# One-core attention and state-space kernel: VectorE's list re-ordered at three places, the first weight copies divided differently, and two attention steps masked by a 0/1 product on GpSimd

## The chip, the core and the metric

The kernel runs on one core of a Trainium2 chip. The metric is the device time of one execution in microseconds (us). Before the change it is 133.39 us, the median of three runs (132.92 to 133.72).

## The reference

Two independent computations over 2048 tokens of width 448; their outputs stand side by side.

```python
# A: 16 heads of 28, each token looks at 8 keys: itself and 7 earlier ones, 2 apart
qkv = (x @ wqkv).reshape(B, S, 3, H, Dh)...
idx = pos[:, None] - (jnp.arange(8) * 2)[None, :]
logits = jnp.where(mask, einsum("bhsd,bhswd->bhsw", q, k[idx]) * scale, -1e9)
a = einsum("bhsw,bhswd->bhsd", softmax(logits), v[idx])... @ wo
# B: a diagonal complex recurrence over the tokens (state h of 448)
Lam_bar = jnp.exp(dt * Lam)
B_bar = ((Lam_bar - 1.0) / Lam)[:, None] * Bmat
h = Lam_bar * h + x[t] @ B_bar.T            # for t in range(2048)
y = 2.0 * real(h @ Cmat.T) + x * Dskip
return concatenate([a, y], -1)
```

## The kernel before

**Tiling.** Even and odd tokens are kept apart ("par" 0 and 1), so that a key distance of 2 is a distance of 1 in either half. Each half has 1024 tokens, in eight blocks b of 128. The attention of a block works on all keys of the same block as a dense 128x128 product per head and lets only a band of 8 through; queries at the start of a block, whose keys lie partly in the block before, are done by a ninth block of borders (b = 8). The recurrence runs over pairs of tokens in two halves hf of 512 pairs, on VectorE's scan instruction, in four groups k of state rows.

**The order.** Every instruction comes from a named step, and the string ORDER lists the steps; each engine executes its part in that order. A token such as `n4.V1` is step n4, on V (VectorE), with PSUM bank pair 1; A is ScalarE, P TensorE, G GpSimd, S the DMA queue of SyncE. The names that matter here:

- `xt0a`, `xt0b`, `xt1` to `xt3` transpose x on TensorE and `xe0a` and so on copy it to xA; `s1v`, `s2v` (lines 486 to 492) copy the v columns of the weights between the two partition halves, and the v steps (`v0e`, `v0o`; lines 351 to 366) multiply by them.
- `k..`, `q..`, `v..` are the projections, `ke`, `qe`, `ve` their copies out of PSUM.
- `s{b}{par}` makes the scores of a block: four mask matmuls (line 645) write a large negative number outside the band into PSUM, sixteen matmuls (line 649) add the products of keys and queries. `x{b}{par}` is the exponential on ScalarE into one of three buffers P (line 671), `a{b}{par}` the product with v (line 680), whose 29th column gives the sum of the weights. `n{b}` divides on VectorE (lines 691, 692), and a step `ot` transposes the result by DMA.
- `b{k}{hf}` makes the input of the recurrence on TensorE (line 727), `be` copies it, `ri` rotates it with two products (lines 742, 743) and two sums (744, 745), `sc` scans (line 755), `ro` rotates back into h (764 to 767). The lines for k = 3 are 747 to 750 and 771 to 774.
- `c1{m}`, `c2{m}` mix the output weights on VectorE (line 540) from products that `tc..` makes on GpSimd or ScalarE (line 534); `g0` to `g2` combine weights on TensorE (782, 784) and `ge0`, `ge1`, `gp2`, `ge2` (809, 819) take them out.
- `y{t}` makes the recurrence's output for 128 pairs of tokens: 7 matmuls with h for the even tokens (line 851), 4 with Gm (854), 7 with h for the odd ones. Ahead of it `xd{t}` (line 841) writes x times Dskip into its bank. `ye` copies the result, `yo` sends it. `w{t}`, `we`, `wo` do the same for the attention.

In front of `y0` and `y1` stand `n8`, `n4`, `n5` in VectorE's list, because their banks are those that a50, a80 and y use. `y5` is the first y that reads the last rotated group, `ro01`.

Of the kernel before, what the change touches and what calls it, by code (L numbers as in the profile page):

```python
# [37 lines left out]
s11.P tc23.G n0.V1 k5t.P0 x11.A k5f.P0 wtx2.S c24.V a10.P1 ri00.V tc21.G qt3.S ke5.A0 s20.P a11.P1 x20.A q7t.P0 xb1.S  # L38
q7f.P0 n1.V1 s21.P qe7.A0 c23.V k6f.P1 x21.A c21.V tc22.G k6t.P1 sc000.V a20.P0 qt4.S ke6.A1 s30.P sc001.V a21.P0
tc20.A kt6.S b20.P1 c22.V x30.A n2.V0 tc25.G kt4.S ro00.V kt5.S s31.P be20.A1 b11.P0 x31.A ot0.S c25.V ri20.V qt5.S  # L40
b31.P1 be11.A0 qt6.S c20.V sc200.V s40.P be31.A1 vg1.S b01.P0 tc12.A tc16.V qt7.S x40.A c16.V c12.V tc15.G ot1.S
sc201.V tc10.A s41.P be01.A0 c10.V a30.P1 a31.P1 c15.V tc14.A b21.P0 vg2.S n3.V1 x41.A tc11.G c14.V ot3.S kb.G c11.V
tc13.A s50.P ot2.S be21.A0 c13.V tc26.G a40.P1 ro20.V x50.A g1.P0 xol.G a41.P1 ge1.A0 s51.P ri11.V g0.P0 x51.A n4.V1
s80.P ge0.A0 c26.V ot4.S a50.P1 sc110.V x80.A a51.P1 wol.S g2.P0 n5.V1 gp2.A0 s60.P ge2.V0 x60.A a80.P1 ot5.S xd1.V0
n8.V1 y1.P0 sc111.V ot8.S xd0.V1 ro11.V s61.P y0.P1 x61.A ri21.V ye1.A0 yo1.S oc0.A a60.P0 sc210.V ye0.A1 yo0.S a61.P0
s70.P n6.V0 w3t.P1 x70.A w3f.P1 sc211.V ot6.S w0f.P0 we3.A1 wo3.S ro21.V w0t.P0 oc1.A s71.P we0.A0 wo0.S w4f.P1 x71.A
ri31.V w5f.P0 w5t.P0 w4t.P1 sc310.V w1t.P2 we4.A1 wo4.S w2t.P3 w1f.P2 we5.A0 wo5.S xd3.V1 w2f.P3 ro31.V we1.A2 wo1.S
a70.P0 we2.A3 wo2.S a71.P0 xd2.V2 y3.P1 n7.V0 xd5.V3 ot7.S ri01.V y2.P2 ye3.A1 yo3.S sc010.V oc2.A sc011.V w6f.P0
# [105 lines left out]
def kernel(  # L154
# [129 lines left out]

    def consts_border():

        k7 = lambda m: m[:, 0:105].rearrange("p (b i) -> p b i", i=15)
        q7 = lambda m: m[:, 0:56].rearrange("p (b j) -> p b j", j=8)
        G.memset(m0, 1.0)
        sel(k7(m1), k7(m0), [[1, 7], [0, 15]], ALU.is_equal, 0.0, 0, -1)  # L290
        sel(k7(m2), k7(m0), [[0, 7], [1, 15]], ALU.is_equal, 0.0, 7, -1)
        G.tensor_tensor(mskb[0:32, 0, 0:105], m1[:, 0:105], m2[:, 0:105], ALU.add)
# [40 lines left out]
    def evac(e, o, i):  # L333
        if e == "A":
            ACT.copy(o, i)  # L335
        elif e == "G":
            G.tensor_copy(o, i)
        else:
            V.tensor_copy(o, i)  # L339
    step = {}  # L340
# [143 lines left out]

    for n, cols in (("v", VC), ("k", KC), ("q", QC)):
        def f(e, u_, cols=cols):
            evac(e, Wt[0:64, 4:7, cols], Wt[64:128, 0:3, cols])
        step["s1" + n] = f

        def f(e, u_, cols=cols):  # L490
            evac(e, Wt[64:128, 3:7, cols], Wt[0:64, 0:4, cols])
        step["s2" + n] = f
    for b_, (n, i, lo, hi) in enumerate((("0a", 0, 0, 3), ("0b", 0, 3, 7), ("1", 1, 0, 7), ("2", 2, 0, 7), ("3", 3, 0, 7))):
        def xt(b_=b_, w=hi - lo):
            return held_by("x")[b_ % 3][:, 0, :].bitcast(BF16)[:, 0:128 * w].rearrange("p (k t) -> p k t", k=w)

        def f(e, u_, xt=xt, i=i, lo=lo, hi=hi):
            for k in range(lo, hi):
                PE.transpose(xt()[:, k - lo, :], xn[:, i, 128 * k:128 * k + 128], eye[:])
# [134 lines left out]
    for place, b in enumerate(SEQ):  # L634
        main_b = b < BORDERS
        ring = 2 * place - (BORDERS in SEQ[:place])
        for par in range(2 if main_b else 1):
            c0, n = (0, 128) if b == 0 else (8, 120)
            Pt_ = Pb[(ring + par) % len(Pb)]

            def f(e, u_, b=b, par=par, n=n, c0=c0):
                s4 = held_by("s")[0]
                tk = slice(128 * b, 128 * b + 128)
                for g in range(4):
                    PE.matmul(s4[:, g, 0:4 * n].rearrange("p (s q) -> p s q", s=4), msk[32 * g:32 * g + 32, 0, :],
                              msk[32 * g:32 * g + 32, 1:2, c0:c0 + n].to_broadcast((32, 4, n)), start=True, stop=False, skip_group_check=True)
# [73 lines left out]
    for hf in range(2):  # L720
        for k in range(4):
# [15 lines left out]
            def f(e, u_, k=k, hf=hf):  # L737
# [8 lines left out]
                else:  # L746
# [2 lines left out]
                    V.tensor_tensor(v[0:64, 0], ra[0:64, 0], ra[64:128, 1], ALU.add)  # L749
                    V.tensor_tensor(v[64:128, 0], ra[64:128, 0], ra[0:64, 1], ALU.subtract)  # L750
            step[f"ri{k}{hf}"] = f
            for i in range(len(ms)):
                def f(e, u_, k=k, hf=hf, i=i):
                    m = k + 4 * i
                    V.tensor_tensor_scan(rs[0][:, i], p["r2"][:, k:k + 1].to_broadcast((128, HALF)), rv[0][:, i],  # L755
                                         0.0 if hf == 0 else ini[:, m:m + 1], ALU.mult, ALU.add)
# [223 lines left out]
```

## Time and profile before

| what | value |
|---|---|
| median of three runs | 133.39 us |
| the profiled execution | 133.22 us |
| its span | 131.4 us |
| granted TensorE clock | 1.00 |
| busy: TensorE, VectorE, ScalarE, GpSimd | 124.2, 107.1, 86.7, 48.1 us |
| GpSimd busy after 77.3 us | none |

The span is the time between the first and the last instruction of the profile. In rows of the timeline the first number is the start, the second the time from the first start to the last end, then come engine, line, operation, output and inputs, shapes and a count; a bracket says how long the engine stood idle before and what ended it. PE is TensorE, PEld its weight loads, DVE VectorE, ACT ScalarE, POOL GpSimd.

### The profile page before, as it was taken

Reading aid. Unit: us, or ns where it says so; the run is one execution under the profiler, and the core shown is the slowest. Engines: PE = TensorE matmul, PEld = TensorE weight load, DVE = VectorE, ACT = ScalarE, POOL = GpSimd, SP = SyncE. Lnnn points to the kernel's source line nnn. Section 1 sums busy time; section 2 is a strip of 40 time slices with the busy share of each in tenths; the row PEclk is TensorE's granted clock in tenths of the full one; section 3 lists DMA queues with packets and bytes.
Section 4 is the critical chain, followed back from the end, with each engine's and each line's share of the span. In section 5 each row is a group of like instructions: output and inputs, shape, how many; then the busy total and the mean of one; then the engine's idle time right before and its main releaser. Section 6 shows DMA issues by size and latency. Waiting matters only on the chain.

```text
span 131.4 us, 3138 instructions
## 1 busy us (share of the span) xinstructions
PE 124.2 (94%) x1226; PEld 63.5 (48%) x1226; DVE 107.1 (81%) x225; ACT 86.7 (66%) x91; POOL 48.1 (37%) x75
## 2 busy tenths in 40 slices
PE   7999999999999999899999998799999999999970
PEld 2654443443444466454445556545644654445540
DVE  2467999999898999999998999999999999870000
ACT  3348878987999879968698967608697523222230
POOL 7998900799851906560077850000000000000000
PEclk9999999999999999999999999999999999999999
DMA  4999998899779995898879967990452652422222
GB/s 98 373 299 223 246 114 164 121 250 204 166 120 200 227 134 86 157 205 200 178 159 148 203 123 260 181 205 14 138 145 71 209 145 70 140 70 72 70 72 80
DMA packets 54594, 20.83 MB, mean 158 GB/s; under 512 B 46830, under 2 KB 54208, under 8 KB 54576
## 3 DMA queue, kind: packets, MB, share of 16 engines
q1 hardware_dynamic: 53424, 18.70, 68.1%
q0 software_dynamic: 656, 1.50, 4.1%
q10 hardware_dynamic: 496, 0.40, 0.9%
q8 instruction: 11, 0.18, 0.6%
q14 instruction: 7, 0.06, 0.2%
HBM read 5.30 MB, written 3.86 MB: 70 GB/s over the span
## 4 chain that ended last, share of the span: by engine, by line
PE 62%; DVE 23%; issue 5%; DMA 3%; POOL 2%; ACT 1%; SPq 0%; DVEq 0%
PE U L362 16%; PE U L851 11%; PE early L362 8%; PE U L727 6%; PE late L851 4%; PE U L854 3%; PE U L360 3%; DVE O L692 3%; DVE natW L540 3%; DMA Wt<-in_A_wqkv_dram 3%; DVE C L540 3%; DVE rs L755 2%; POOL wtmp L534 2%; PE late L362 2%; PE early L360 2%
## 5 line engine op out<-in xcount | busy, mean ns | idle before, releaser
L671 ACT ACTIVATE P<-s 128x1920 bf16<-128x1920 f32 (+1 forms) x16 | 28.6, 1785 | 5.7 <-PE s L649 5.6
L727 PE MATMUL U<-xB,WT 128*128 128x512 bf16 x98 | 22.3, 380 | 0.0
L362 PE MATMUL U<-Wt,xA 128*128 128x448 bf16 x90 | 19.9, 355 | 0.7 <-DVE O L692 0.4
L362 PEld LDWEIGHTS <-xA 128*128 128x128 bf16 x144 | 12.9, 98 | 14.9 <-issue 4.4
L335 ACT CAST ys<-U 128x896 bf16<-128x896 f32 (+1 forms) x11 | 9.5, 871 | 12.0 <-PE U L851 9.2
L534 POOL TENSOR_SCALAR wtmp<-CT,p_pah 128x448 f32<-128x448 bf16 x6 | 12.6, 2107 | 11.2 <-DVE natW L540 6.4
L851 PEld LDWEIGHTS <-h 128*128 128x128 bf16 x105 | 10.0, 98 | 9.2 <-DVE U L841 0.2
L727 PEld LDWEIGHTS <-WT 128*128 128x128 bf16 x98 | 9.2, 98 | 10.7 <-DMA xB<-in_B_x_dram 0.2
L362 PE MATMUL early<-Wt,xA 128*128 128x448 bf16 x54 | 11.8, 354 | 0.0
L335 ACT CAST u<-U 128x1024 bf16<-128x1024 f32 (+1 forms) x8 | 7.2, 905 | 4.6 <-PE U L727 4.5
L692 DVE TENSOR_TENSOR O<-U,rcs 128x896 bf16<-128x896 f32 (+1 forms) x9 | 9.8, 1091 | 0.3
L851 PE MATMUL U<-natW,h 128*128 128x448 bf16 x42 | 9.0, 353 | 0.1
L755 DVE TENSOR_TENSOR_SCAN rs<-p_r,rv 128x512 bf16<-128x512 f32 x7 | 9.0, 1304 | 0.0
L755 DVE TENSOR_TENSOR_SCAN rs<-p_r,ini,rv 128x512 bf16<-128x512 f32 x7 | 8.8, 1275 | 0.0
L680 PE MATMUL U<-Vt,P 128*128 128x29 bf16 x256 | 8.2, 176 | 0.6 <-DVE O L692 0.6
L680 PEld LDWEIGHTS <-P 128*128 128x128 bf16 x256 | 7.6, 96 | 2.0 <-issue 0.7
L335 ACT CAST ys<-late 128x896 bf16<-128x896 f32 (+2 forms) x6 | 4.3, 718 | 6.1 <-PE late L851 5.6
L362 PE MATMUL U<-wo,OT 128*128 128x448 bf16 x36 | 7.6, 353 | 0.0
L851 PE MATMUL U<-C,h 128*128 128x448 bf16 x35 | 7.4, 353 | 0.0
L534 POOL TENSOR_SCALAR wtmp<-CT,p_pag 128x448 f32<-128x448 bf16 x2 | 4.2, 2081 | 8.4 <-DVE C L540 8.4
L339 DVE COPY Wt<-Wt 64x1344 bf16<-64x1344 bf16 (+1 forms) x5 | 3.7, 736 | 4.1 <-DMA Wt<-in_A_wqkv_dram 4.1
L335 ACT CAST Nx<-U 128x896 bf16<-128x896 f32 x7 | 6.4, 908 | 1.0 <-PE U L360 1.0
(198 smaller groups left out, 233.9 us busy)
## 6 DMA issues: line engine op xcount, KB each, us to landing
out_dram<-ys SPq DMA_DIRECT2D x12, 224.0 KB, 2.5
tmpB<-in_A_x_dram SPq DMA_DIRECT2D x4, 224.0 KB, 3.6
xo<-in_B_x_dram POOLq DMA_DIRECT2D x1, 896.0 KB, 6.7
out_dram<-ys SPq DMA_DIRECT2D x7, 112.0 KB, 1.8
Wt<-in_A_wqkv_dram SPq DMA_DIRECT2D x1, 672.0 KB, 6.0
wo<-in_A_wo_dram SPq DMA_DIRECT2D x2, 336.0 KB, 4.4
natW<-in_B_B_re_dram SPq DMA_DIRECT2D x1, 336.0 KB, 6.0
natW<-in_B_B_im_dram SPq DMA_DIRECT2D x1, 336.0 KB, 7.3
```

What stands on the lines that cost most here:

```text
L335: ACT.copy(o, i)
L360: PE.matmul(ps(u_)[j], x()[r, 3, c], w()[r, 3], start=first, stop=not first, skip_group_check=True)
L362: PE.matmul(ps(u_)[j], x()[:, 4 * j + k, c], w()[:, 4 * j + k], start=(k == 0 and first), stop=(k == 2 and not first), skip_group_check=True)
L534: (G if e == "G" else V).tensor_scalar(view(held_t[name][:]), src(), scale(), None, ALU.mult)
L540: V.scalar_tensor_tensor(view(dst()), src(), scale(), view(t[:]), ALU.mult, ALU.add)
L671: ACT.activation(pv[:, :, :, c0:128], s4[:, :, 0:4 * n].rearrange("p g (s q) -> p g s q", s=4), ACTF.Exp, scale=SCALE)
L680: PE.matmul(U[u_][:, q, 29 * hd:29 * hd + 29], P[:, hd // 4, hd % 4, :], Vt[:, b, q, hd, :], start=(hd == 0), stop=(hd == H - 1), skip_gro ...
L692: V.tensor_tensor(O[0:n, :].rearrange("p (t h d) -> p t h d", t=2, h=H), av[0:n, :, :, 0:DH], rc.unsqueeze(3).to_broadcast((n, 2, H, DH)), ...
L727: PE.matmul(U[u_][:, j, :], WT[:, i, 128 * m:128 * m + 128], xB[:, i, HALF * hf:HALF * hf + HALF], start=(i == 0), stop=(i == 6))
L755: V.tensor_tensor_scan(rs[0][:, i], p["r2"][:, k:k + 1].to_broadcast((128, HALF)), rv[0][:, i], 0.0 if hf == 0 else ini[:, m:m + 1], ALU.m ...
L851: PE.matmul(ps[:, 0:D], hb[:, m, lo:lo + 128], C1()[:, m, :] if par else natW[:, m, 0:D], start=(m == 0 and par == 0), stop=(m == 6 and pa ...
L854: PE.matmul(ps[:, 0:D], xB[:, k, tk], Gm[:, k, :], start=False, stop=(k == 3), skip_group_check=True)
```

## The change

1. **Start.** `xe0a` moves from ScalarE to VectorE. `s1v` copies one of its three rows of 448 columns (64 partitions); the other two become a step `s0v` on ScalarE, behind `xe0b`.
2. **ri00 in two.** `rp00` is its two products, `rq00` its two sums, and `n1` stands between them.
3. **ri11 and sc110.** `ri11` moves behind `n4`; `sc110` moves behind `n5`, `ge2`, `xd1` and `n8`.
4. **Products.** `s60` and `s70` leave out their four mask matmuls, so their first product matmul starts the sum. New steps `m60` and `m70` on GpSimd multiply P in place, 16 x 120 columns, by a 0/1 tile `band`, repeated over the 16 heads. `x60` and `x70` come before them, `a60` and `a70` behind. `band` is made at the start of GpSimd's step `cob` by a memset and two selects of 128x128.

```diff
-spin spin spin spin spin spin sps sps sps xt0a.P xt0b.P xe0a.A co0.G s1v.V xe0b.A sps sps v0e.P0 nw.S s2v.V nt.G sps
+spin spin spin spin spin spin sps sps sps xt0a.P xt0b.P xe0a.V co0.G s1v.V xe0b.A s0v.A sps sps v0e.P0 nw.S s2v.V nt.G
...
+    band = t_([128, 128], BF16, "band")
+    STEPS = {tok.partition(".")[0] for tok in ORDER.split()}
...
+        G.memset(band[:], 1.0)
+        sel(band[:], band[:], [[1, 128]], ALU.is_ge, 0.0, 0, -1)
+        sel(band[:], band[:], [[-1, 128]], ALU.is_ge, 0.0, 7, 1)
...
-            evac(e, Wt[0:64, 4:7, cols], Wt[64:128, 0:3, cols])
+            hi = 5 if cols == VC else 7
+            evac(e, Wt[0:64, 4:hi, cols], Wt[64:128, 0:hi - 4, cols])
...
+    step["s0v"] = lambda e, u_: evac(e, Wt[0:64, 5:7, VC], Wt[64:128, 1:3, VC])
...
-                for g in range(4):
+                masked = f"m{b}{par}" not in STEPS
+                for g in range(4 if masked else 0):
                     PE.matmul(s4[:, g, 0:4 * n]..., msk[32 * g:32 * g + 32, 0, :], ...
...
-                                  Qt[...], start=False, stop=(s == 3), skip_group_check=True)
+                                  Qt[...], start=(s == 0 and not masked), stop=(s == 3), skip_group_check=True)
...
+            def f(e, u_, P=Pt_, c0=c0):
+                pv = P[:].rearrange("p s g q -> p (s g) q")[:, :, c0:128]
+                G.tensor_tensor(pv, pv, band[:, c0:128].unsqueeze(1).to_broadcast((128, H, 128 - c0)), ALU.mult)
+            step[f"m{b}{par}"] = f
...
+            for nm, part in (("rp", 0), ("rq", 1)):
+                def f(e, u_, k=k, part=part):
+                    if part == 0:
+                        for o, s in ((ra, tab[:, 0, k, :]), (rb, tab[:, 1, k, :])):
+                            V.tensor_tensor(o[:], u[:, k:k + 5:4, :], s.unsqueeze(1).to_broadcast((128, 2, HALF)), ALU.mult)
+                    else:
+                        V.tensor_tensor(rv[0][:, 0], ra[:, 0], rb[:, 1], ALU.add)
+                        V.tensor_tensor(rv[0][:, 1], ra[:, 1], rb[:, 0], ALU.subtract)
+                step[f"{nm}{k}{hf}"] = f
```

How this stands in the engines' lists, at three places. VectorE at the start, behind its memsets, before:

```order
L339 COPY Wt<-Wt 64x3x448
L339 COPY Wt<-Wt 64x4x448
L339 COPY xA<-x_145 128x7x128
L339 COPY xA<-x_144 128x7x128
L339 COPY Wt<-Wt 64x3x448
```

and after, where the helper's copies are line 345:

```order
L345 COPY xA<-x_144 128x3x128
L345 COPY Wt<-Wt 64x448
L345 COPY Wt<-Wt 64x4x448
L345 COPY xA<-x_146 128x7x128
L345 COPY xA<-x_145 128x7x128
```

A copy of x (xe0a) has come in ahead, and the first weight copy (s1v) has a third of its columns.

VectorE around `n5` and `n8` before: c26 (natW), the scan sc110, n5 (rcs and the first O), ge2, xd1, n8 (a memset, rcs, the second O), the scan sc111, xd0.

```order
L540 SCALAR_TENSOR_TENSOR natW<-CT,p_sah,wtmp_125 128x448
L755 SCALAR_TENSOR_TENSOR rs_131<-p_r_321,ini,rv_130 128x512
L691 RECIPROCAL rcs<-U_94 128x32
L692 TENSOR_TENSOR O_1374<-U_94,rcs 128x896
L819 TENSOR_TENSOR Gm<-U_93,part 64x448
L841 TENSOR_TENSOR U_93<-xo 128x448
L688 MEMSET O_1435 32x448
L691 RECIPROCAL rcs<-U_94 56x32
L692 TENSOR_TENSOR O_1435<-U_94,rcs 56x896
L755 SCALAR_TENSOR_TENSOR rs_131<-p_r_321,ini,rv_130 128x512
L841 TENSOR_TENSOR U_94<-xo 128x448
```

The same place after (the scan is now line 778, the division 705 and 706, xd 864):

```order
L548 SCALAR_TENSOR_TENSOR natW<-CT,p_sah,wtmp_126 128x448
L705 RECIPROCAL rcs<-U_95 128x32
L706 TENSOR_TENSOR O_1378<-U_95,rcs 128x896
L842 TENSOR_TENSOR Gm<-U_94,part 64x448
L864 TENSOR_TENSOR U_94<-xo 128x448
L702 MEMSET O_1436 32x448
L705 RECIPROCAL rcs<-U_95 56x32
L706 TENSOR_TENSOR O_1436<-U_95,rcs 56x896
L778 SCALAR_TENSOR_TENSOR rs_132<-p_r_323,ini,rv_131 128x512
L864 TENSOR_TENSOR U_95<-xo 128x448
```

The scan sc110 has moved from ahead of n5 to behind n8. Ahead of these rows n4 and ri11 have changed places in the same way.

GpSimd's end of the list after: the copy of the border keys, the last product for c26, two loads of x and Dskip, and the two new products; before, the load of `flag` followed the two loads directly.

```order
L343 COPY Kb<-Kt 128x840
L542 TENSOR_SCALAR wtmp_126<-CT,p_pah 128x448
L931 DMA xo<-in_B_x_dram 128x8x448
L932 DMA xo<-in_B_Dskip_dram 128x448
L687 TENSOR_TENSOR P_84<-P_84,band 128x16x120
L687 TENSOR_TENSOR P_83<-P_83,band 128x16x120
L957 TENSOR_LOAD flag
```

Only these two instructions are new there; they wait for ScalarE's exponential, and a60 and a70 for them.

More of the change, by code (lines that the diff above doesn't have):

```diff
@@ L37 @@
 k2f.P1 qe4.A0 sc100.V s10.P qt2.S ke2.A1 b00.P0 sc101.V x10.A kt2.S ro10.V tc24.G kt7.S a00.P1 be00.A0 a01.P1 wtx6.S
[L38 to L41, printed above, removed]
+s11.P tc23.G n0.V1 k5t.P0 x11.A k5f.P0 wtx2.S c24.V a10.P1 rp00.V tc21.G qt3.S ke5.A0 s20.P a11.P1 x20.A q7t.P0 xb1.S
@@ L44 @@
[L44 to L48, printed above, removed]
@@ L49 @@
-ye2.A2 yo2.S ro01.V w6t.P0 w7t.P1 we6.A0 wo6.S w7f.P1 xda.V2 y5.P3 we7.V1 wo7.S gu1.V xd6.V0 gu2.P1 y6.P0 ye5.A3 yo5.S
-gu3.V1 xd4.V1 flag.V xdb.V3 y4.P1 ye6.A0 yo6.S ya7.P0 ye4.A1 yo4.S yb0.P2 ye7.A0 yb1.P3 yf0.A2 yf1.A3 yp7.A yq7.S
+tc13.A s50.P ot2.S be21.A0 c13.V tc26.G a40.P1 ro20.V x50.A g1.P0 xol.G a41.P1 ge1.A0 s51.P g0.P0 x51.A n4.V1 ri11.V
+s80.P ge0.A0 c26.V ot4.S a50.P1 x80.A a51.P1 wol.S g2.P0 n5.V1 gp2.A0 s60.P ge2.V0 x60.A m60.G a80.P1 ot5.S xd1.V0 n8.V1
+sc110.V xd0.V1 y1.P0 sc111.V ot8.S ro11.V s61.P y0.P1 x61.A ri21.V ye1.A0 yo1.S oc0.A a60.P0 sc210.V ye0.A1 yo0.S
@@ new lines @@
+a61.P0 s70.P n6.V0 w3t.P1 x70.A m70.G w3f.P1 sc211.V ot6.S w0f.P0 we3.A1 wo3.S ro21.V w0t.P0 oc1.A s71.P we0.A0 wo0.S w4f.P1
+x71.A ri31.V w5f.P0 w5t.P0 w4t.P1 sc310.V w1t.P2 we4.A1 wo4.S w2t.P3 w1f.P2 we5.A0 wo5.S xd3.V1 w2f.P3 ro31.V we1.A2
+wo1.S a70.P0 we2.A3 wo2.S a71.P0 xd2.V2 y3.P1 n7.V0 xd5.V3 ot7.S ri01.V y2.P2 ye3.A1 yo3.S sc010.V oc2.A sc011.V
+w6f.P0 ye2.A2 yo2.S ro01.V w6t.P0 w7t.P1 we6.A0 wo6.S w7f.P1 xda.V2 y5.P3 we7.V1 wo7.S gu1.V xd6.V0 gu2.P1 y6.P0
+ye5.A3 yo5.S gu3.V1 xd4.V1 flag.V xdb.V3 y4.P1 ye6.A0 yo6.S ya7.P0 ye4.A1 yo4.S yb0.P2 ye7.A0 yb1.P3 yf0.A2 yf1.A3
@@ L51 @@
+yp7.A yq7.S
 """
@@ L649, in f @@
                         PE.matmul(s4[:, g, s * n:s * n + n], Kt[32 * g:32 * g + DH, par, s, tk],
-                                  Qt[32 * g:32 * g + DH, par, s, 128 * b + c0:128 * b + 128], start=False, stop=(s == 3), skip_group_check=True)
+                                  Qt[32 * g:32 * g + DH, par, s, 128 * b + c0:128 * b + 128], start=(s == 0 and not masked), stop=(s == 3), skip_group_check=True)
             def f_b(e, u_):
```

8 lines of the change are left out of this document (5 added, 3 removed).

## The prediction

> **What bounds the kernel now.** I read the page's line of busy times first, then the chain of waits, then the timeline of the stretches in which the chain changes its engine.
>
> ```profile
> PE 124.2 (94%) x1226; PEld 63.5 (48%) x1226; DVE 107.1 (81%) x225; ACT 86.7 (66%) x91; POOL 48.1 (37%) x75
> ...
> PE 62%; DVE 23%; issue 5%; DMA 3%; POOL 2%; ACT 1%; SPq 0%; DVEq 0%
> ```
>
> TensorE looks like the bound, but its 94% is an average. The chain of waits, whose shares are the second line, runs over TensorE up to 46.5 us, mostly over VectorE from there to 84.9 us, and over TensorE again to the end. The next rows say what lies under the second and third part: a row of the windows (the numbers ahead of the engines' names in its heading are PE, PEld, DVE, ACT, POOL busy), and the end of VectorE's list with the TensorE matmuls behind it.
>
> ```profile
> 76.98:112.84 35.86, 34.36 (x400) 18.80 (x399) 34.90 (x58) 21.27 (x22) 0.25 (x1) 1.00 0.53 139
> ```
>
> ```profile
> 112.08 0.43 DVE L766 TENSOR_TENSOR h<-ra,rb 128x512 bf16<-128x512 bf16 x1
> 112.42 0.42 DVE L767 TENSOR_TENSOR h<-ra,rb 128x512 bf16<-128x512 bf16 x1
> ...
> 113.38 1.49 PE L851 MATMUL late<-natW,h 128*128 128x448 bf16 x7
> ```
>
> For 35.86 us VectorE is busy 34.90: it has no gap that another order could fill. At 112.51 it ends the last block of h that the step y5 reads first, and y5 starts at 113.38. From there to 127 us TensorE runs without a pause. **So there are two limits**: TensorE may arrive at y5 early, but by at most 113.38 - 112.51 = 0.87 us, unless VectorE's list itself ends earlier; and every microsecond by which VectorE's list grows beyond 0.87 is paid in full.
>
> **The change part by part.** The sum is made against the profiled execution, 133.22 us, of which the span is 131.4; the median of the three runs is 133.39, so both agree within 0.2.
>
> *First weight copies.* Row 5.87 is the transposes of xt1, 6.77 the matmuls of v0o.
>
> ```profile
> 4.43 1.01 ACT L335 COPY xA<-x 128x384 bf16<-128x384 bf16 x2 [1.26 <-PE x L499]
> ...
> 4.99 1.72 DVE L339 COPY Wt<-Wt 64x1344 bf16<-64x1344 bf16 x2 [3.24 <-DMA Wt<-in_A_wqkv_dram]
> ...
> 5.87 0.55 PE L499 MATMUL x<-eye,tmpB 128*128 128x128 bf16 x7
> ...
> 6.77 0.73 PE L362 MATMUL U<-Wt,xA 128*128 128x448 bf16 x3 [0.35 <-DVE Wt L339]
> ```
>
> Before, VectorE copies 1344 and 1792 columns in 1.72 us, and v0o waits 0.35 for the second. After, VectorE does xe0a in its idle time ahead of the DMA, then 448 and 1792 columns: 2240/3136 of 1.72 is 1.23, ready at 6.22. ScalarE does xe0b (512 columns, half of 1.01) and then s0v, 896 columns at the same rate, 0.9 to 1.0 us: 4.85 + 0.50 + 1.0 = 6.35. TensorE is busy with xt1 until 6.42, so v0o starts there: 0.35 us less. Most of this is stopped at the next gate: the weight load of b30 waits for the transposed xB.
>
> ```profile
> 32.64 1.37 PEld L727 LDWEIGHTS <-WT 128*128 128x128 bf16 x7
> ```
>
> It starts at 32.64, when that transfer has landed, while TensorE is held by the matmuls ahead until 32.99. So TensorE keeps 0 to 0.35 us of it.
>
> *Split ri00.* Row 50.87 is the first add of ri00, 51.79 the reciprocal of n1, 53.31 the step k6f, which needs n1's bank.
>
> ```profile
> 50.87 0.66 DVE L744 TENSOR_TENSOR rv<-ra,rb 128x512 bf16<-128x512 bf16 x1
> ...
> 51.79 0.34 DVE L691 RECIPROCAL rcs<-U 128x32 f32<-128x32 f32 x1
> ...
> 53.31 1.30 PE L362 MATMUL U<-Wt,xA 128*128 128x448 bf16 x6 [0.40 <-DVE O L692]
> ```
>
> n1 starts 0.92 earlier, so TensorE's wait of 0.40 goes. VectorE does the same work in both orders.
>
> *ri11 behind n4, sc110 behind n8.* Rows 80.51 (a50), 83.67 (a80) and 84.87 (y1) are TensorE's; 82.38 (gp2) and 82.98 (x60) are ScalarE's.
>
> ```profile
> 76.98 0.69 DVE L742 TENSOR_TENSOR ra<-u,tab 128x1024 bf16<-128x1024 bf16 x1
> ...
> 78.98 0.35 DVE L691 RECIPROCAL rcs<-U 128x32 f32<-128x32 f32 x1
> ...
> 80.37 0.67 DVE L540 SCALAR_TENSOR_TENSOR natW<-CT,p_sah,wtmp 128x448 bf16<-128x448 bf16 x1
> 80.51 0.96 PE L680 MATMUL U<-Vt,P 128*128 128x29 bf16 x32 [0.56 <-DVE O L692]
> 80.97 1.28 DVE L755 TENSOR_TENSOR_SCAN rs<-p_r,ini,rv 128x512 bf16<-128x512 f32 x1
> 82.16 0.33 DVE L691 RECIPROCAL rcs<-U 128x32 f32<-128x32 f32 x1
> ...
> 82.38 0.53 ACT L335 COPY part<-U 64x448 f32<-64x448 f32 x1 [0.64 <-PE U L782]
> ...
> 82.98 1.77 ACT L671 ACTIVATE P<-s 128x1920 bf16<-128x1920 f32 x1
> ...
> 83.67 1.06 PE L682 MATMUL U<-Vb,P 105*56 105x29 bf16 x32 [0.80 <-DVE O L692]
> 84.17 0.63 DVE L841 TENSOR_TENSOR U<-xo 128x448 f32<-128x448 bf16 x1
> 84.87 1.50 PE L851 MATMUL U<-natW,h 128*128 128x448 bf16 x7
> 84.95 0.43 DVE L688 MEMSET O<- 32x448 f32 x1
> ...
> 86.81 1.27 DVE L755 TENSOR_TENSOR_SCAN rs<-p_r,ini,rv 128x512 bf16<-128x512 f32 x1
> ```
>
> n4 (80.37 - 78.98 = 1.4 us) now runs ahead of ri11 and ends at 78.4, so the wait of 0.56 goes. Without the scan (82.16 - 80.97 = 1.19) n5, ge2 and xd1 end 1.2 earlier, the wait of 0.80 moves with them, and y1 starts near 83.75 instead of 84.87. gp2 needn't wait 0.64 for TensorE, ends near 82.4, and x60 runs from there to 84.2. n8 (1.9 us, 84.95 to 86.81) runs 83.7 to 85.6, sc110 after it. VectorE's list is only re-ordered, so its end stays at 112.51: **all orders together can give 0.87 us at y5**, and the more than 1 us gained at y1 meets that limit.
>
> *Two products on GpSimd.* s60 and s70 lose four mask matmuls each.
>
> ```profile
> 88.44 0.32 PE s L645 x4
> ...
> 88.97 1.43 PE U L851 x7
> ...
> 92.48 0.80 PE U L680 x32
> ```
>
> In this piece of the chain the first row is a step's four mask matmuls, the second the start of y0, the third a60. So 2 x 0.32 us of TensorE go, worth nothing where TensorE then waits for VectorE. What is added is a product of 128x1920 elements between x60 and a60, and one between x70 and a70. No row has this operation. Nearest are small GpSimd products, and copies beside VectorE work:
>
> ```profile
> L268 POOL TENSOR_TENSOR msk<-Gm 32x128 bf16<-32x128 bf16 x1 | 0.4, 414 | 0.1
> L292 POOL TENSOR_TENSOR mskb<-Gm 32x105 bf16<-32x105 bf16 x1 | 0.4, 376 | 0.1
> ```
>
> ```profile
> 49.73 2.30 POOL L534 TENSOR_SCALAR wtmp<-CT,p_pah 128x448 f32<-128x448 bf16 x1 [3.46 <-DVE natW L540]
> ...
> 57.68 1.40 POOL L534 TENSOR_SCALAR wtmp<-CT,p_pah 128x448 f32<-128x448 bf16 x1 [0.98 <-DVE natW L540]
> 57.89 1.09 DVE L692 TENSOR_TENSOR O<-U,rcs 128x896 bf16<-128x896 f32 x1
> ...
> 63.01 0.43 DVE L744 TENSOR_TENSOR rv<-ra,rb 128x512 bf16<-128x512 bf16 x1
> ...
> 71.59 1.29 POOL L337 COPY Kb<-Kt 128x840 bf16<-128x840 bf16 x1
> ```
>
> ```profile
> 72.05 1.90 DVE L540 SCALAR_TENSOR_TENSOR C<-CT,p_sag,wtmp 128x448 bf16<-128x448 bf16 x2
> ```
>
> Length: 38 ns for 23 elements is 1.65 ns each and 0.20 fixed, so 0.20 + 1920 x 1.65 ns = 3.4 us. Bounds: 1.8 us at the copy's rate (from VectorE's end at 72.05 + 0.04 to 72.88, 0.79 us for 840, 0.94 ns), 6.0 us at 1.40/448 = 3.1 ns.
>
> Making the 0/1 tile adds three 128x128 instructions to GpSimd's constants; the step behind them has 4.27 us of idle time ahead of it, so they cost nothing:
>
> ```profile
> 42.39 3.88 POOL L534 TENSOR_SCALAR wtmp<-CT,p_pah 128x448 f32<-128x448 bf16 x2 [4.27 <-DMA CT<-in_B_C_re_dram]
> ```
>
> What VectorE loses: the two L540 behind 72.05 take 1.90 where two take 1.28 (80.37 shows 0.67 for one), so the copy cost VectorE 0.62 of its own 0.79 us. The 0.66 at 50.87 against 0.43 at 63.01 is 0.23 beside a product with a scalar. The L692 at 57.89, whose large operand lies in PSUM, loses nothing, and GpSimd beside it takes its shortest 1.40. So a VectorE instruction that reads two SBUF tensors stops while GpSimd streams, and one like L692 doesn't. Bounds for one product: 0.23 us (as a scalar one), or all of its length and more, 6.0 us. I take its whole length, 3.4, since the copy, which moves bf16 to bf16 as the product does, cost four fifths of its own; what n8 and n6 cover is taken off.
>
> m60 starts at 84.3, in n8, and holds until 87.7; sc110 is due at 85.6: 2.1 us. xd0 stands behind sc110, and y0 on TensorE behind xd0. y0 (92.48 - 88.97 = 3.5 us) then runs 89.5 to 93.1, s70 is done at 94.2 and x70 at 96.0.
>
> ```profile
> 93.83 0.33 DVE L691 RECIPROCAL rcs<-U 128x32 f32<-128x32 f32 x1
> ```
>
> a60, now behind y0 at 93.1 (92.48 before), doesn't wait for m60. n6, at 93.83 + 2.1, begins as m70 does and covers 1.4; sc211 then waits from 97.4 to 99.4: 2.0 us. Together 4.05 us. y5 starts at 112.51 + 4.05 = 116.56 instead of 113.38, +3.2. What is behind (y6 needs xd6, further on in VectorE's list) moves alike. The start's 0.35 and the 0.64 of masks vanish in the wait at y5. **Sum: 133.2 + 3.2 = 136.4 us.**
>
> The Trainium skill, "SBUF — State Buffer", section "SBUF: two separate sides", says that a GpSimd instruction reading SBUF and a VectorE instruction with two SBUF inputs exclude each other for the whole instruction. The trace agrees that L692 is spared, but beside the product at 49.73 VectorE lost 0.23 of its last 1.2 us, not all; the copy at 71.59 is nearer to the rule. "GPSIMD Engine Reference", section 3.1, gives about 2.6 cycles per element for two inputs at 1.2 GHz: an estimate by that page of 4.2 us for a product, by which the sum would be 138.0 us.
>
> **Rivals.**
> 1. *The products run beside VectorE without a cost* (faster). Then the order's gain stands: 133.22 - 0.87 = 132.35 us. It decides if both products together take under 0.2 us from VectorE. L692 speaks for it, the 0.23 and 0.62 against it. 9%.
> 2. *One short stall per product*, 0.23 to 0.62 as in the rows: 0.5 to 1.2 us less 0.87, so 132.9 to 133.6. That needs the stream to be buffered ahead as the scalar one seems to be; the product has over four times the elements. 13%.
> 3. *GpSimd gives way instead* and a60 waits. Beside VectorE the scalar product grows from 1.40 to 2.30, up to 9 us for a product here: m60 ends at 93.3, TensorE, early, reaches a60 near 91.4, so 1.9 late; a70 likewise, n7 with it, and y5 about 1 us late: 134.3. 8%.
> 4. *Longer or uncovered holds*: 3.4 twice without n8 and n6 gives 133.2 + 6.8 - 0.87 = 139.2; 6.0 twice with cover gives 9.2 us of stall and 141.6. 15%.
>
> **How the numbers follow.** The forecast, holds of 2.8 to 4.2 us partly covered, has 55%: 135 to 138. A measurement here can tell about 0.5%, 0.67 us, from no change. Faster by more: rival 1, 0.09. Within: rival 2, 0.13. Slower: 0.78. The range runs from 133.0, which leaves out rival 1 and a corner of rival 2, to 139.6, which leaves out the upper half of rival 4.
>
> **What would show it.** Right: VectorE's first instruction with two SBUF inputs behind n8 (sc110) lasts or waits about 2 us more, likewise sc211; y1 starts near 83.8; a wait of TensorE before y0 and before y5, both for VectorE; ro01 ends near 116.9. Wrong: scans at 1.28 us beside the product and VectorE's list ending at 112.8 or before (rival 1), or TensorE waiting at a60 and a70 for GpSimd (rival 3). That the order didn't do what it says would show as waits at a50 and k6f still there.

## The result and the profile after

The changed kernel takes 136.95 us (median of 5 runs, 136.47 to 137.25) against 133.04 us for the kernel before in the same job (five runs; the 133.39 above is the median of the first three of them): a ratio of 1.0275, 95% interval 1.0253 to 1.0296. The forecast was 136.4. Ratios leave out the runs that were more than 1.5% longer than the fastest of their kernel, two of twelve in e1 and three of six in e14; in e11, where it would be three of four, single times stand in place of a ratio.

The profiled execution took 137.25 us, its span is 135.4. The page's line of busy times, and the group of the scans that stand on VectorE's list:

```profile
PE 126.2 (93%) x1218; PEld 64.1 (47%) x1218; DVE 111.4 (82%) x226; ACT 87.0 (64%) x91; POOL 57.2 (42%) x80
...
L778 DVE TENSOR_TENSOR_SCAN rs<-p_r,ini,rv 128x512 bf16<-128x512 f32 x7 | 13.2, 1893 | 0.0
```

VectorE's busy time grew from 107.1 to 111.4 us with one instruction more. 4.3 us of the growth are in a single group: these seven scans took 8.8 us before (1275 ns each) and take 13.2 now (1893 each). A stalled instruction counts as busy, so the loss shows in durations and not as idle time. The timelines of GpSimd (two rows) and VectorE (five) say which scans:

```profile
83.85 3.94 POOL L687 TENSOR_TENSOR P<-P,band 128x1920 bf16<-128x1920 bf16 x1 [6.82 <-ACT P L680]
...
96.57 3.82 POOL L687 TENSOR_TENSOR P<-P,band 128x1920 bf16<-128x1920 bf16 x1 [8.77 <-ACT P L680]
```

```profile
85.12 1.08 DVE L706 TENSOR_TENSOR O<-U,rcs 56x896 bf16<-56x896 f32 x1
86.13 2.75 DVE L778 TENSOR_TENSOR_SCAN rs<-p_r,ini,rv 128x512 bf16<-128x512 f32 x1
...
89.32 1.27 DVE L778 TENSOR_TENSOR_SCAN rs<-p_r,ini,rv 128x512 bf16<-128x512 f32 x1
...
96.32 1.09 DVE L706 TENSOR_TENSOR O<-U,rcs 128x896 bf16<-128x896 f32 x1
97.33 4.13 DVE L778 TENSOR_TENSOR_SCAN rs<-p_r,ini,rv 128x512 bf16<-128x512 f32 x1
```

sc110 lasts 2.75 us and sc211 4.13, where both lasted 1.28 before and sc111, with no product beside it, lasts 1.27: holds of 1.47 and 2.85 us, 4.32 together. Both end 1.1 us behind the end of the product beside them (88.88 against 87.79, 101.46 against 100.39), so each ran all but 0.2 us of its own length only when GpSimd was done. n8 and n6 (L706), whose large operand lies in PSUM, took their usual 1.08 and 1.09 beside a product.

One delay was not foreseen. On VectorE (first row) xd1 waits for a load, and on TensorE (second) y1 waits for xd1:

```profile
83.50 0.63 DVE L864 TENSOR_TENSOR U<-xo 128x448 f32<-128x448 bf16 x1 [0.71 <-DMA xo<-in_B_Dskip_dram]
```

```profile
84.19 1.94 PE L874 MATMUL U<-natW,h 128*128 128x448 bf16 x7 [0.81 <-DVE U L864]
```

Before, xd1 began at 84.17; now its turn comes at 82.79, ahead of a transfer that it used to find landed. At the end of VectorE's list, and at y5 on TensorE:

```profile
117.06 0.43 DVE L789 TENSOR_TENSOR h<-ra,rb 128x512 bf16<-128x512 bf16 x1
```

```profile
117.57 1.49 PE L874 MATMUL late<-natW,h 128*128 128x448 bf16 x7
```

The block of h that y5 needs ends at 117.49 instead of 112.51, 4.98 later: 4.32 of holds, 0.71 of xd1's wait, 0.05 the other way. y5 starts 0.08 behind it, where 0.87 lay between them before: 4.98 - 0.87 + 0.08 = 4.19 us later. The waits of TensorE in this part of the program:

```profile
PE U L874 <- DVE U L864: 1.9, 2, 1.1
PE U L368 <- DVE O L706: 1.3, 1, 1.3
PE U L368 <- ACT OT L341: 0.7, 1, 0.7
PE U L696 <- DVE O L706: 0.5, 1, 0.5
```

No line names P: a60 and a70 never wait for GpSimd. TensorE pays for VectorE's lateness at w0f (which waits for n6's bank), at y1 and y3 (both for U from L864) and at w6f, which waits for the result of n7 after its transposing transfer and ScalarE's copy (OT):

```profile
114.70 1.31 PE L368 MATMUL U<-wo,OT 128*128 128x448 bf16 x6 [0.69 <-ACT OT L341]
```

From there TensorE reaches y5 in 2.87 us, as it did before (110.52 to 113.38, 2.86). Its matmuls don't wait at y0 and y5, as was forecast; only the weight load of y5 waits, 0.25 us, for h. So TensorE got to y5 just when h was ready, and VectorE's list sets both, since n7 stands on it too (its end came at 110.80 instead of 105.81, 4.99 later).

### The profile page after: what moved, and what is told of

It reads as the page before. It is cut to its first block, busy times and chain, and to the rows that moved or that the text cites. A ratio compares the mean times of both kernels' runs of the same rounds, so it can differ in the third digit from the quotient of the medians.

```text
span 135.4 us, 3130 instructions
## 1 busy us (share of the span) xinstructions
PE 126.2 (93%) x1218; PEld 64.1 (47%) x1218; DVE 111.4 (82%) x226; ACT 87.0 (64%) x91; POOL 57.2 (42%) x80
## 4 chain that ended last, share of the span: by engine, by line
PE 49%; DVE 28%; DMA 8%; issue 5%; POOL 5%; ACT 1%; DVEq 0%; POOLq 0%
PE U L368 14%; DVE rs L778 10%; PE early L368 8%; PE U L741 6%; DMA xo<-in_B_Dskip_dram 5%; PE U L874 5%; POOL wtmp L542 4%; DVE O L706 3%; PE U L366 3%; DMA OT<-O 3%; PE x L516 2%; PE late L874 2%; PE U L877 2%; PE x L507 2%; PE early L366 1%
## 5 line engine op out<-in xcount | busy, mean ns | idle before, releaser
L542 POOL TENSOR_SCALAR wtmp<-CT,p_pah 128x448 f32<-128x448 bf16 x6 | 13.1, 2180 | 9.5 <-DVE natW L548 4.9
L687 POOL TENSOR_TENSOR P<-P,band 128x1920 bf16<-128x1920 bf16 x2 | 7.8, 3878 | 15.6 <-ACT P L680 15.6
L778 DVE TENSOR_TENSOR_SCAN rs<-p_r,ini,rv 128x512 bf16<-128x512 f32 x7 | 13.2, 1893 | 0.0
L706 DVE TENSOR_TENSOR O<-U,rcs 128x896 bf16<-128x896 f32 (+1 forms) x9 | 9.8, 1090 | 0.3
L874 PE MATMUL U<-C,h 128*128 128x448 bf16 x35 | 8.0, 371 | 0.0
L368 PEld LDWEIGHTS <-OT 128*128 128x128 bf16 x48 | 4.3, 98 | 7.1 <-issue 2.5
```

The source lines that it names most:

```text
L368: PE.matmul(ps(u_)[j], x()[:, 4 * j + k, c], w()[:, 4 * j + k], start=(k == 0 and first), stop=(k == 2 and not first), skip_group_check=True)
L542: (G if e == "G" else V).tensor_scalar(view(held_t[name][:]), src(), scale(), None, ALU.mult)
L687: G.tensor_tensor(pv, pv, band[:, c0:128].unsqueeze(1).to_broadcast((128, H, 128 - c0)), ALU.mult)
L706: V.tensor_tensor(O[0:n, :].rearrange("p (t h d) -> p t h d", t=2, h=H), av[0:n, :, :, 0:DH], rc.unsqueeze(3).to_broadcast((n, 2, H, DH)), ...
L874: PE.matmul(ps[:, 0:D], hb[:, m, lo:lo + 128], C1()[:, m, :] if par else natW[:, m, 0:D], start=(m == 0 and par == 0), stop=(m == 6 and pa ...
```

## The experiments

**The theory**: a GpSimd instruction that reads SBUF and a VectorE instruction that reads two SBUF tensors shut each other out for the whole instruction; the products cost what of their length is not covered by other VectorE work. **Rivals**: the new order of the list costs the time, with or without products (R1); any GpSimd work at that place does, reading or writing (R2); only GpSimd instructions with two inputs do (R3).

**e1: list and start without the products** (R1).

```
-x60.A m60.G a80.P1
+x60.A a80.P1
-x70.A m70.G w3f.P1
+x70.A w3f.P1
```

> The changed kernel without m60 and m70; s60 and s70 have their mask matmuls back. Theory H (a VectorE instruction with two SBUF inputs stands still while a GpSimd product streams; the products cost their overlap with such instructions): VectorE's list ends where it ended before, a little later for the 0.7 us that xd1 waits for the load of x, so 132.4 to 133.0 us, both scans near 1.28 us. Rival R1 (the re-ordering, sc110 behind n8, costs the time): 136 us or more.

133.59 us, ratio 1.0023 (0.9996 to 1.0049). The scans took 1.27 to 1.29, y1 began at 83.16, h's block ended at 112.12 (L789, 111.69 and 0.43) and y5 began at 113.00. On TensorE:

```profile
94.95 1.29 PE L368 MATMUL U<-wo,OT 128*128 128x448 bf16 x6 [1.31 <-DVE O L706]
```

R1 falls: by the interval the order costs 0.5% at most. The profiled run (132.95) lies in the expected range, the median above it. Nor does the order bring the 0.87 us: the 1.7 us gained at y1 (84.87 before) are given back here, where w0f waits for n6, and 0.38 are left at y5, which stands 0.88 behind VectorE's block: TensorE sets it here.

**e2: the products in the order of before.** ORDER and the first weight copies as before, with `m60.G` behind `x60.A` and `m70.G` behind `x70.A`.

> The order of before with nothing but the two products added behind x60 and x70 and the masks of s60 and s70 left out. H: m60 runs from 84.8 and holds sc111 for about 1.7 us; m70 takes over behind sc211 near 96.4 and holds the first product of ro21 for about 3.7 us; VectorE's list ends 5.4 us later, less 0.87 of slack: 137.6 us. R1 (the order costs the time): 133.0 us.

137.89 us, ratio 1.0341 (1.0308 to 1.0374). The holds are there without the new order, on whatever stands beside the product: sc111 took 2.88 us beside m60. For m70, GpSimd's row and two of VectorE's:

```profile
96.81 4.80 POOL L686 TENSOR_TENSOR P<-P,band 128x1920 bf16<-128x1920 bf16 x1 [8.30 <-ACT P L679]
```

```profile
96.72 1.28 DVE L777 TENSOR_TENSOR_SCAN rs<-p_r,ini,rv 128x512 bf16<-128x512 f32 x1
98.03 4.13 DVE L786 TENSOR_TENSOR ra<-rs,tab 128x1024 bf16<-128x1024 bf16 x1
```

Here the scan had begun 0.09 us ahead of the product and took its usual 1.28; the product took 1 us more than the other (4.80 against 3.82), and the next VectorE instruction, a product of two SBUF tensors that takes 0.68 alone, took 4.13. Whoever begins first goes through.

**e3: the products on VectorE.** `m60.V` and `m70.V`, same places.

> The changed kernel with m60 and m70 on VectorE at the same places of the order. H: VectorE's own time for one is about 1.15 us (0.60 for 1024 elements of the same type), so its list grows by 2.3 us instead of 4.3: 134.5 to 135.2 us, faster than with GpSimd. If GpSimd's work cost VectorE nothing, this would be slower than the changed kernel by 2 us: 139 us.

136.19 us, ratio 1.0222 (1.0201 to 1.0243).

```profile
84.41 1.16 DVE L687 TENSOR_TENSOR P<-P,band 128x1920 bf16<-128x1920 bf16 x1 [1.03 <-ACT P L680]
...
98.50 1.16 DVE L687 TENSOR_TENSOR P<-P,band 128x1920 bf16<-128x1920 bf16 x1 [0.59 <-ACT P L680]
```

Both products cost VectorE 2.32 us of its own work, as expected, and 1.6 us of waiting for ScalarE's exponentials, which the expectation left out, so its 134.5 to 135.2 were missed. By the ratios (1.0222 against 1.0275, intervals apart) it is still faster than the changed kernel: what was handed to GpSimd cost VectorE more than doing it.

**e4: GpSimd only writes** (R2). Two memsets of the same tile in place of the product.

```
-G.tensor_tensor(pv, pv, band[...], ALU.mult)
+for _ in range(2):
+    G.memset(pv, 1.0)
```

> The changed kernel with the product replaced by two memsets of ones over the same 16x120 columns of P, so GpSimd writes as many elements but reads none; the mask matmuls are kept. The attention weights of the even tokens in blocks 6 and 7 are thereby all ones. H, in the form that the reads are what holds VectorE: the scans stay near 1.28 us and the time is that of the kernel without products, 132.4 to 133.2 us. Rival R2 (any GpSimd instruction at that place holds VectorE): scans of 2 to 4 us and 135 to 137 us.

133.24 us, ratio 1.0012 (0.9994 to 1.003).

```profile
83.64 3.46 POOL L688 MEMSET P<- 128x1920 bf16 x2 [6.97 <-ACT P L680]
```

```profile
85.09 1.27 DVE L779 TENSOR_TENSOR_SCAN rs<-p_r,ini,rv 128x512 bf16<-128x512 f32 x1
```

GpSimd is as busy at the same place, and the scan in the middle of it takes 1.27: R2 falls. It is the reading that holds.

**e9: one select with one input** (R3).

```
-G.tensor_tensor(pv, pv, band[...], ALU.mult)
+sel(pv, pv, [[0, H], [1, 128 - c0]], ALU.is_ge, 0.0, c0, -1)
```

> The changed kernel with one select with one input (P, written back in place; no band) in place of each product. It masks only one side of the band, so of the two attention steps' mask the other side is left out. Asks whether the hold comes with GpSimd's reading of SBUF or only with a second input. My theory (VectorE's scans, both of whose inputs are read with SBUF among them, stop while GpSimd reads) says: sc110 and sc211 are held again, for a time that follows from the select's own length, so the kernel stays at 134 to 138 us, and each hold ends about 1.1 us behind the end of the GpSimd instruction. The rival, that only a two-input GpSimd instruction holds VectorE for its length (the one-input ones in the kernel before cost VectorE's instructions 0.2 to 0.6 us apiece), says scans of 1.3 to 1.9 us and 133.2 to 134.5 us.

133.03 us, ratio 0.9996 (0.9977 to 1.0015): by its time R3's result, and the range of the theory missed. The rows of the second select:

```profile
94.11 1.90 POOL L256 TENSOR_SCALAR_AFFINE_SELECT P<-P 128x1920 bf16<-128x1920 bf16 x1 [8.46 <-ACT P L680]
```

```profile
95.18 1.91 DVE L778 TENSOR_TENSOR_SCAN rs<-p_r,ini,rv 128x512 bf16<-128x512 f32 x1
```

A select takes 1.90 us, half a product. The scan is held for 0.63, and ends at 97.09, 1.08 us behind the select (96.01), as behind the product. n6 covered the rest. So the time alone could not decide, and e13 doubles the select.

**e13: two selects**, one for each side of the band.

> The changed kernel with two selects with one input (one for each side of the band) in place of each product; nothing is left out. In the run with one select its length was 1.90 us, the scan sc211 beside it lasted 1.91 instead of 1.28, and both scans ended 1.08 us behind the end of the select, just as they did behind the product; the time was that of before only because n8 and n6 covered nearly all of 1.90. If reading by GpSimd holds VectorE whether it has one input or two, two selects (3.8 us) end at 87.5 and 99.9 us or so, sc110 lasts 2.3 to 2.8 us and sc211 3.6 to 4.1 unless it gets in between the two, and the time is 136 to 137.3 us. If the one-input instruction lets VectorE through in the main, the scans keep to 1.3 to 1.9 us and the time is 133 to 134 us.

136.40 us, ratio 1.0226 (1.021 to 1.0243): R3 falls too. The second select at the first place, and VectorE beside it:

```profile
85.74 4.86 POOL L256 TENSOR_SCALAR_AFFINE_SELECT P<-P 128x1920 bf16<-128x1920 bf16 x1
```

```profile
85.92 1.27 DVE L779 TENSOR_TENSOR_SCAN rs<-p_r,ini,rv 128x512 bf16<-128x512 f32 x1
...
87.63 1.27 DVE L779 TENSOR_TENSOR_SCAN rs<-p_r,ini,rv 128x512 bf16<-128x512 f32 x1
88.94 2.21 DVE L788 TENSOR_TENSOR ra<-rs,tab 128x1024 bf16<-128x1024 bf16 x1
```

The select got no turn while VectorE ran three instructions back to back (4.86 us instead of 1.90), then had one, and `ra` was held 1.5 us. At the second place `ra` was held 1.5 us again and sc211 0.2 (1.48 us). The time is the expected one; the instructions held are mostly not the two scans that the expectation named.

**e8: each product in four pieces.**

```
+for i in range(4):
+    pi = pv[:, 4 * i:4 * i + 4]
+    G.tensor_tensor(pi, pi, band[...], ALU.mult)
```

> The changed kernel with each product cut into four instructions of four heads each (128 x 480 elements), nothing left out. If VectorE is shut out instruction by instruction, it gets in between two pieces: the scans sc110 and sc211 run after at most one piece each (some 1 us more than 1.28), the product as a whole takes longer by what VectorE does in between, and the time falls to 134 to 135.5 us. If instead GpSimd keeps what it has taken as long as it has work in its queue, the scans are held as before, 1.5 and 2.9 us, and the time stays at 136.5 to 138.

136.91 us, ratio 1.028 (1.0255 to 1.0305).

```profile
83.76 7.51 POOL L689 TENSOR_TENSOR P<-P,band 128x480 bf16<-128x480 bf16 x4 [6.82 <-ACT P L680]
```

```profile
85.91 1.27 DVE L780 TENSOR_TENSOR_SCAN rs<-p_r,ini,rv 128x512 bf16<-128x512 f32 x1
...
88.92 1.40 DVE L789 TENSOR_TENSOR ra<-rs,tab 128x1024 bf16<-128x1024 bf16 x1
90.24 1.58 DVE L790 TENSOR_TENSOR rb<-rs,tab 128x1024 bf16<-128x1024 bf16 x1
```

VectorE does get in between the pieces: sc110 isn't held, and the four pieces take 7.51 us. But `ra` and `rb` (0.69 and 0.68 alone) are held by a piece each, 1.61 us here and, at the second place, 2.5 with the scan's 2.21: some 4.2 us in all, as before. The expected gain missed: pieces move the hold to other instructions of the same list and don't shorten it.

**e11: sc110 ahead of xd1**, so that the scan is done when the product starts.

> The changed kernel with one move: the scan sc110 stands ahead of xd1 instead of behind n8, so it starts near 82.6 to 83.5 us, before the product m60 does. Nothing is left out. If the instruction that starts first keeps its place, the scan takes 1.3 us, m60 starts or stretches up to 1 us later, xd1 hides its wait for the load of x, and the held one is then sc111 or xd0 behind n8, by 0.5 to 1.5 us; the VectorE list ends 0 to 0.8 us earlier than in the changed kernel, so 136.1 to 137.0 us. If GpSimd always wins, sc110 is held from 83.9 to 87.8 and the time is 137.5 to 139.

One run took 137.07 us, three 140.16 to 141.32. The profiled one, at 140.16, on VectorE and on TensorE:

```profile
83.53 4.25 DVE L864 TENSOR_TENSOR U<-xo 128x448 f32<-128x448 bf16 x1
```

```profile
87.84 2.80 PE L874 MATMUL U<-natW,h 128*128 128x448 bf16 x7 [4.84 <-DVE U L864]
```

The scan took 1.27, as expected of the first to begin, but m60 then began at 83.48, 0.05 us ahead of xd1, and xd1 (0.63 alone) was held to 87.78. TensorE stands for 4.84 us, since y1 waits for xd1. The expectation had named the instructions behind n8 as the next ones to be held; in this execution the one directly behind the scan was. The run of 137.07 has no profile, so that it escaped this hold is likely and not shown.

**e12: the loads of x and Dskip earlier on GpSimd's queue**, to price xd1's 0.71 us.

```
-c13.V tc26.G a40.P1 ro20.V x50.A g1.P0 xol.G
+c13.V xol.G tc26.G a40.P1 ro20.V x50.A g1.P0
```

> The changed kernel with GpSimd's loads of x and Dskip issued two of its instructions earlier (some 3 us). Nothing is left out. In the changed kernel xd1 waited 0.71 us for that transfer, TensorE 0.81 us for xd1, and TensorE's clock was at 0.5 to 0.8 for 5 us from there. If that wait sits on VectorE's list as the holds do, it is worth its 0.71 us in full: y1 at 83.4 to 83.5, the last group of the list 0.6 to 0.7 us earlier, 136.0 to 136.5 us. If the time that it gives is taken back by a longer hold (n8 would then end earlier, while the product ends where it did, at 87.8), sc110 lasts 3.4 instead of 2.75 us, and the time stays at 136.8 to 137.2. I lean to the second, since the end of the product is set by ScalarE's x60 and not by VectorE. The clock drop should go in either case if the wait brings it about.

140.55 us, ratio 1.0546 (1.0515 to 1.0577), outside of both expectations. VectorE:

```profile
82.77 1.09 DVE L706 TENSOR_TENSOR O<-U,rcs 128x896 bf16<-128x896 f32 x1 [1.86 <-DMA OT<-O]
83.78 0.61 DVE L842 TENSOR_TENSOR Gm<-U,part 64x448 bf16<-64x448 f32 x1
84.42 3.38 DVE L864 TENSOR_TENSOR U<-xo 128x448 f32<-128x448 bf16 x1
```

xd1 no longer waits for its load. But n5 now waits 1.86 us for the transfer that empties its O buffer (why that came later is not shown), so xd1 comes behind m60 (83.50) and is held for 2.8, and TensorE waits for it again. What xd1's 0.71 us is worth by itself stays open.

**e6: the start alone**, list and masks as before.

```
-sps xt0a.P xt0b.P xe0a.A co0.G s1v.V xe0b.A sps
+sps xt0a.P xt0b.P xe0a.V co0.G s1v.V xe0b.A s0v.A sps
```

> The kernel before with only the start changed: one copy of x moved to VectorE and the first weight copy split between VectorE and ScalarE; list and masks as before. Nothing is left out. The prediction gave the start 0 to 0.35 us of TensorE's time, most of it stopped at b30. The profile of the changed kernel had v0o at 6.80 (before 6.77), so no gain: 132.9 to 133.5 us and v0o at 6.4 to 6.8. A gain of 0.35 us (132.85) would mean that the first step was read rightly and its profile was off.

132.80 us, ratio 0.9962 (0.9948 to 0.9975). The profiled execution was the longest of its five runs, 133.25 us, and shows no gain at v0o (third row):

```profile
4.65 1.31 PE L367 MATMUL U<-Wt,xA 128*128 128x448 bf16 x3
...
6.07 0.87 PE L506 MATMUL x<-eye,tmpB 128*128 128x128 bf16 x7
6.78 0.73 PE L367 MATMUL U<-Wt,xA 128*128 128x448 bf16 x3
```

In the profiles of eight other experiments with this start v0o began at 6.41 to 6.45, as the prediction had it, in e9 and e8 at 6.59 and 6.69, in the changed kernel at 6.80. The length of v0e, the first row, doesn't sort them: it is 1.31 us here and in the changed kernel, but also in e11, where v0o began at 6.43. What decides is open. The other four runs, 132.66 to 132.97, fit a gain of 0.35 or a little more.

**e10: e1, with two memsets of VectorE's list (0.24 and 0.43 us) on GpSimd.**

```
-V.memset(O[32:64, :].bitcast(F32), 0.0)
+G.memset(O[32:64, :].bitcast(F32), 0.0)
-V.memset(Gm[64:128, 3, :], 0.0)
+G.memset(Gm[64:128, 3, :], 0.0)
```

> The list and the start of the changed kernel without products, and two memsets of VectorE's list (0.24 and 0.43 us) put on GpSimd, which is idle there. Nothing is left out. By the prediction's first step two limits end at y5: VectorE's list, and TensorE, which had 0.87 us to spare before the change. The list without products came out 0.38 us earlier at y5; 0.67 us less on VectorE makes 1.05, of which TensorE lets 0.87 through: y5 at 112.5 us, a wait of y5 for VectorE gone or under 0.2 us, and 132.3 to 132.9 us. If GpSimd's writes hold VectorE as its reads do, the gain is gone and the time is 133.2 to 133.8.

132.75 us, ratio 0.9972 (0.9945 to 0.9999), as expected. h's block on VectorE and y5 on TensorE:

```profile
111.12 0.43 DVE L789 TENSOR_TENSOR h<-ra,rb 128x512 bf16<-128x512 bf16 x1
```

```profile
112.44 1.49 PE L874 MATMUL late<-natW,h 128*128 128x448 bf16 x7
```

VectorE is done at 111.55 and y5 starts at 112.44, 0.89 behind it, so TensorE sets y5. It is 0.56 us earlier than in e1, which is what w0f is earlier (94.39 against 94.95), with 0.67 us of its wait for n6 left.

**e14: e10, with the division n6 ahead of the scan sc210**, so that w0f needn't wait for it.

```
-a60.P0 sc210.V ye0.A1 yo0.S a61.P0 s70.P n6.V0
+a60.P0 ye0.A1 yo0.S a61.P0 s70.P n6.V0 sc210.V
```

> The kernel with the re-ordered list and start, no products, and two memsets on GpSimd, with one more move: the division n6 stands ahead of the scan sc210. Nothing is left out. In the run without the move y5 started at 112.44 and no longer waited for VectorE, whose last group ended at 111.55; TensorE's largest wait was 0.67 us at w0f for n6. If y5 is now bound by TensorE, as the prediction's first step has it, that wait goes, and since VectorE's end leaves 0.9 us all of it comes through: y5 at 111.8 us, median 131.9 to 132.4 us. If VectorE's list still bounds, y5 stays at 112.3 to 112.5 and the median at 132.6 to 132.9.

Ratio 0.9867 (0.9848 to 0.9887) by three of its six runs, 131.32, 131.56 and 131.89 us. The three others took 133.5 to 134.3, and the median of all six is 132.71. So it is the fastest version in half of its executions; what sets the others apart was not settled. In the profiled one, at 131.89, the two of TensorE's groups that matter:

```profile
92.90 2.44 PE L368 MATMUL U<-wo,OT 128*128 128x448 bf16 x12
...
112.19 1.50 PE L874 MATMUL late<-natW,h 128*128 128x448 bf16 x7
```

w0f follows w3f in one row of twelve matmuls, with no wait between. In this execution y1 waited 0.9 us for xd1, VectorE's block of h (111.70 and 0.43) ended at 112.13, and y5 follows 0.06 behind it. From w6f (109.23) it took 2.96 us instead of 2.86, and its weight load waited 0.37 for h: the bound is VectorE's list again. Neither expectation fits: xd1 waited 0.73 us for its load here, and in e10 it did not.

## Why the prediction was right

Its mechanism and its direction held, and its size in the main: +3.2 us forecast, and 137.25 - 133.22 = 4.0 between the profiled executions, 3.9 between the medians. That the size came so near is partly luck (steps 5 and 6). Step by step:

1. *Two limits.* Right. In the changed kernel both meet at y5, 0.08 us behind VectorE's block; e10 shows TensorE's limit alone and e14 VectorE's. The base of the sum was a little too good: the order with no products lets y5 gain 0.38 (e1), not 0.87, since w0f's wait for n6 takes TensorE's lead away. In the sum this is no loss, since y5 can't start ahead of VectorE's block.
2. *First weight copies.* v0o's 0.35 us came in e1, and b30 didn't stop them: its matmuls began there at 32.48 instead of 32.83. The gain in e6, 0.46 us by the medians (0.33 to 0.69), lies at the top of the forecast 0 to 0.35 or above. In the profile of the changed kernel v0o began at 6.80, so it gained nothing there.
3. *Split ri00.* The wait at k6f is gone.
4. *ri11 and sc110.* The waits at a50 and a80 went or shrank (0.5 at L696). y1 came at 84.19 instead of 83.75, for xd1's load; in e1, where it had landed, at 83.16.
5. *Products.* Their length was 3.94 and 3.82 us for 3.4: 12% too short an estimate from the small product's row. The holds were 1.47 for m60 (2.1 forecast) and 2.85 for m70 (2.0). m60 began 0.45 earlier and n8, behind xd1's wait, ended 0.5 later than forecast, so n8 covered more; n6 gave way to the scan 0.76 us after m70's start, where 1.4 of cover were counted, and m70 was 0.4 longer. The two errors nearly cancel, 4.32 for 4.05, and that is luck. (The two forecast holds, 2.1 and 2.0, add up to 4.1.)
6. *What the sum lacked.* xd1's wait for its load, 0.71 us of VectorE's time. With 0.27 more of holds it explains why the end of the list came at 117.49 and not at 116.56 (0.98 of 0.93).

The term that was off, then, is not the hold but what n8 and n6 cover of it, in both directions, and a transfer that was late once its reader came early. Where TensorE waits was off too: at w0f, y1, y3 and w6f instead of y0 and y5, in the end for the same engine.

Of the rivals, the first two (no cost, a short stall) are gone with the 1.47 and 2.85. The third, that GpSimd gives way, is true of the mechanism (e2, e8, e13), but in the changed kernel the products began first and a60 and a70 never waited; its price of up to 9 us for a product was also a little low by its own rows (2.30 us for 448 elements make 9.9 for 1920). The fourth overstated the length.

The products run as the Trainium skill, "SBUF — State Buffer", section "SBUF: two separate sides", has it: the one that starts first keeps the other out for the whole instruction (e2, e11), n8 and n6 (one input in PSUM) are spared, and so is everything beside e4's writes. Beside the scalar product at 49.73, which the prediction set against that rule, it is not the whole instruction: the add at 50.87, which reads two SBUF tensors, ends at 51.53, half a microsecond ahead of GpSimd's end at 52.03. The single input alone doesn't explain this, since the scan beside a select with one input ended 1.08 us behind the select (e9). No experiment changed that scalar product, so why it lets go earlier stays open. The estimate of 4.2 us for a product from the Trainium skill's "GPSIMD Engine Reference", section 3.1, was nearer to the 3.8 to 3.9 measured than the prediction's 3.4, and overstates it by some 8%.

## What to carry to other kernels

Work handed from a busy VectorE or TensorE to an idle GpSimd can cost more than it saves if VectorE has instructions with two SBUF inputs due in that time: here 2.32 us of work (e3) became 4.3 us of holds. Whether a VectorE instruction with a single SBUF input, such as a copy, is held too was not tried. Look for the loss in the duration of the other engine's instructions, not in its idle time; and what only writes, such as a memset, could be handed over at no cost here (e4, e10). After a re-ordering, look at which transfers and which bank the instructions that come earlier now meet (xd1's load, n6 at w0f), because the gain is given back there.

## What the runs showed of the hardware that was not expected

- **Whoever begins first keeps the way, and back-to-back VectorE work starves GpSimd.** A select of 1.90 us took 4.86 beside three VectorE instructions in a row (e13), and the third piece of a product waited likewise, 3.91 us instead of 1.09 (e8). A small lead is enough: xd1 took 4.25 us when the product began 0.05 us ahead of it (e11), and 0.63 in the changed kernel, where xd1 was ahead by 0.35.
- **TensorE's clock fell after some of its waits, and not the longest.** In the windows of the changed kernel (the numbers are as in the prediction's row; the clock is the third from the end), TensorE waits in the first and runs at about half clock a little later; in e11 the clock is at half already within its wait of 4.84 us:

```profile
83.40:84.19 0.79, 0.00 (x1) 0.01 (x1) 0.63 (x1) 0.37 (x1) 0.34 (x1) 1.00 1.16 308
...
85.00:87.00 2.00, 2.00 (x7) 0.81 (x6) 1.97 (x3) 0.00 (x0) 2.00 (x1) 0.53 1.71 210
```

```profile
85.00:87.84 2.84, 0.00 (x1) 0.01 (x1) 2.78 (x1) 0.00 (x0) 2.29 (x1) 0.50 0.66 81
```

  It doesn't follow every wait: in the changed kernel TensorE also waited 1.32 us at w0f and 1.05 at y3, in e1 1.31 at w0f, and the clock stayed at 1.00. What it costs is not settled: the profiled execution of the changed kernel, at a mean clock of 0.987, was the longest of the five, 137.25 us against 136.47 to 136.95 for the four at 1.00. The Trainium skill, "TensorE: Matmul & The Clock Gate", Part 1, "The HAM clock gate", has the gate close after an idle window of about 3.4 us, on a window that runs freely. That a wait of 0.8 us was followed by a fall and a longer one was not would fit the second part; that 0.8 us was enough is shorter than the Trainium skill says. What decides it was not settled.
